# Splitting a first matmul of three chunks into two passes of one and a half, with the hidden layout turned to match

## The chip, the cores and the metric

The kernel runs on one core of one Trainium2 chip. The metric is the device time of that core in microseconds (us). Three runs of the kernel before took 957.19, 957.78 and 957.98 us; the median is 957.78.

The engines are called PE (TensorE, matmuls), PEld (its weight loads), ACT (ScalarE), DVE (VectorE), POOL (GpSimd, which also issues the adding DMAs) and SP (SyncE, which issues loads and stores).

## The reference

The input `x` is (8, 4224, 192). A light convolution with 7 taps per head (8 heads of 24 channels, softmax over the taps) is followed by a block that normalises each row, multiplies by a 192 x 768 weight, takes relu, multiplies by a 768 x 192 weight and adds the row back:

```python
out = np.einsum('hk,bskhg->bshg', w, x_unf)          # 7 causal taps
xn = (x - mu) / np.sqrt(var + 1e-06) * g_ln
ch = np.maximum(xn @ w_ch1, 0.0) @ w_ch2
return (x + ch).astype(np.float32)
```

All arithmetic is fp32. Inputs arrive as 64-bit words in part, which the kernel's first stage converts; the change does not touch that.

## The kernel before

Rows are worked in 18 groups; a full group holds 128 partitions x 16 rows (2048 rows). For each group: taps on ACT (the first two) and DVE (the other five), a 32x32 transpose on DVE (`yt`), the first matmul into the hidden tile, relu, the second matmul, a transpose back, a scale by 1/sigma (ACT) and an addition into the output in DRAM by DMA. Taps of the next group run while this group's matmuls do. Everything is written out in the order in which each engine is to do it (`tc.manual_schedule()`); semaphores are put in wherever two instructions touch the same bytes.

Groups 3 to 17 are the 15 "mixed" groups. In them both matmuls use a Winograd form of Strassen's scheme, with 7 products of quarter matrices instead of 8. The first matmul (`up_mixed`, L611) has rows in two halves and the 768 hidden columns in two halves of three chunks of 128 (`FC = 3`). It multiplies 32-row slices of `yt`: four slices `q` = 0 to 3 run at the same time, each into its own PSUM bank. `rows_of_tiles` (L525) issues them. There are eight PSUM banks; `take_set` (L125) gives four at a time, so there are two sets, X and Y, that take turns.

The three chunks don't fit into one bank of 512 columns (3 x 256 = 768). So the seven products are done in two passes: pass `one` with one chunk (256 columns per bank) and pass `two` with two chunks (512 columns). In each pass the seven products alternate between X and Y. After a product the set is emptied in one of two ways. `evict` (L642) is an ACT copy or relu into the hidden tile. `close` adds a set to what is already in the hidden tile: either DVE adds straight out of PSUM (L648), or ACT evicts into a scratch place and POOL issues an adding DMA from there (L609, `add_by_dma`). Quarters of the hidden tile are called `c11`, `c12`, `c21`, `c22`. Scratch for pass one is the part of `c12` and `c22` that pass two will fill later; scratch for pass two are the rooms `cs` and `tb` of other tiles.

ACT also does the relu of `c11` and `c22` in place (L655). `c12` gets its relu in the eviction, `c21` in `lower_sum` (L806), where DVE also subtracts `c11` from it, as the second matmul needs.

The hidden tile `ht[g]` is one room of SBUF for all groups. In a mixed group its layout is `h e f q j t`: half of rows, half of columns, chunk `f`, slice `q`, then 256 columns. A chunk of a quarter is thus 1024 elements in a row, one run per partition.

The second matmul (`down_fast`, L818) has seven products again (L835). Each runs over three output slices `c`, and for each over chunks in the order 2, 0, 1. It takes six banks one after the other: products called with 0 use `banks[2 * c]`, those called with 1 use `banks[2 * c + 1]`. With X as banks X0 to X3 and Y as Y0 to Y3, the former write X0, X2, Y0 and the latter X1, X3, Y1. After each output slice ACT copies the bank out (L841), and one to three entries of a list `work` follow on ACT: relus that are left, scales of the group before, and the first two taps of the group after the next. Between the products DVE does three `half_sum`s on quarters of the hidden tile (L799).

`ahead` (L981) finishes the group before on DVE (`finish_fast`: addition of two rooms, then transposes), and `up_mixed` calls it between the passes. `pending` is the chain on POOL that works out 1/sigma for two groups (`root`, L450); it is run in two parts from `up_mixed` of the even groups, in POOL's order between the adding DMAs. On DVE the order in `up_mixed` is: `ahead`, 28 tap instructions, `lower_sum` of chunk 2, 3 taps, `close` of `c21`, `lower_sum` of chunks 0 and 1, 9 taps, transpose.

Of the kernel before, what the change touches and what calls it, by code (L numbers as in the profile page):

```python
# [16 lines left out]
def kernel(  # L17
# [475 lines left out]
    def hidden_tile(g):  # L493
        n = groups[g][2]

        if fast[g]:
            ht[g] = room.rearrange(
                "p (h e f q j t) -> p h e f q j t", h=2, e=2, f=FC, q=NQ, t=width(g)
            )
        else:  # L500
            ht[g] = room[:, 0 : NF * NQ * n * C].rearrange(
                "p (f j q t) -> p f j q t", f=NF, q=NQ, t=C
            )
# [5 lines left out]
    def evict_up(g, f, src):  # L509
# [4 lines left out]
        elif width(g) == C:  # L514
            dst = of_products(g)[:, :, f // FC, f % FC].rearrange("p h q j t -> p q h (j t)")
            src = src.rearrange("p q (h w) -> p q h w", h=2)
        else:
            dst = ht[g][:, :, f // FC, f % FC].rearrange("p h q j t -> p q j h t")
# [92 lines left out]
    def up_mixed(g, ahead, pending):  # L611


        W = HJ * C
        last = g + 1 == NG
        assert groups[g][2] == 2 * HJ and PAIR * W == 512 and FC == PAIR + 1
# [3 lines left out]
        s1, s2, s3, s4 = ysums[g]  # L620
        done = groups[g - 1][2]

        class Pass:
            def __init__(self, f0, f1, chain, other):
                self.n, self.chain, self.other = f1 - f0, chain, other
                self.b11, self.b12, self.b21, self.b22 = quarters_of_w1(f0, f1)
                self.t = [v[:, :, P * f0 : P * f1] for v in (w1sums[:, k] for k in range(3))]
                (self.c11, self.c12), (self.c21, self.c22) = [
                    [a[:, h, e, f0:f1].rearrange("p f q j t -> p f q (j t)") for e in range(2)]
                    for h in range(2)  # L630
                ]

            def product(self, to, left, right, first=True, end=True):
                rows_of_tiles(to, left, right, first, end, True)

            def seen(self, banks, f=None):
                src = banks[:, :, 0 : self.n * W] if f is None else banks[:, :, W * f : W * f + W]
                return src.rearrange("p q (f w) -> p f q w", w=W)

            def evict(self, banks, dst, relu=False, f=None):  # L640
                src = self.seen(banks, f)
                nc.scalar.activation(dst, src, AF.Relu) if relu else nc.scalar.copy(dst, src)  # L642

            def close(self, c, banks, part=None, f=None):


                if part is None:
                    nc.vector.tensor_tensor(c, c, self.seen(banks), op=ALU.add)  # L648
                    return
                self.evict(banks, part, f=f)  # L650
                whole = "p f q w -> p (f q w)"
                add_by_dma(c.rearrange(whole), part.rearrange(whole))

            def relu(self, c):
                nc.scalar.activation(c, c, AF.Relu)  # L655

        def parts(pool, tag):

            room = pool.tile([P, J * D], F32, tag=tag, name=f"parts_{tag}{g}")
            return room.rearrange("p (f q w) -> p f q w", q=NQ, w=W)  # L660
# [11 lines left out]
        one, two = Pass(PAIR, FC, X, Y), Pass(0, PAIR, Y, X)  # L672
        p = one
        p.product(X, a11, p.b11, True, False)
        p.evict(X, p.c11)
        p.product(Y, a12, p.b21)
        p.close(p.c11, Y, two.c12[:, 0:1])
        next(pending, None)
        p.product(X, s2, p.t[0], False, False)
        p.evict(X, p.c21)  # L680
        p.product(Y, s3, p.t[1], True, False)
        p.evict(Y, p.c22)
        p.product(X, s1, p.b12, False, False)
        p.close(p.c22, X, two.c12[:, 1:2])
        next(pending, None)
        p.product(Y, a22, p.t[2], False)
        p.close(p.c21, Y, two.c22[:, 0:1])
        p.product(X, s4, p.b22, False)
        p.evict(X, p.c12, True)

        next(ahead)
        p = two
        rooms = parts(cpool, "cs"), parts(bpool, "tb")
        p.product(Y, a11, p.b11, True, False)
        p.evict(Y, p.c11)
        p.product(X, a12, p.b21)
        if last:
            p.close(p.c11, X)
        else:
            for f in range(PAIR):  # L700
# [390 lines left out]
```

## Time and profile before

| | |
|---|---|
| median of the runs | 957.78 us |
| the profiled execution | 959.62 us, span 957.5 us |
| clock granted to PE | 1.0 |
| PE busy | 950.6 us, 99% of the span |
| DVE busy | 890.7 us, 93% |
| ACT busy | 696.6 us, 73% |
| POOL busy | 338.4 us, 35% |
| DMA, queue of POOL | 106.25 MB, 59.8% of 16 engines' span |
| first matmul of one mixed group, in the chain of waits | 27.96 us |
| second matmul of one mixed group, in the chain of waits | 27.44 us |

The page gives, for a group of equal instructions, busy time, mean duration of one in nanoseconds, and the idle time of the engine just before them with what ended it. In a timeline a line has start, duration, engine, line of the kernel, operation, tiles and shapes; a bracket at its end is the idle time before it and the releaser. An fp32 matmul shows as two records. Since four slices run at once, a matmul record lasts longer (374 ns) than the step at which new ones start.

### The profile page before, as it was taken

To read this page: it belongs to the slowest core of one execution; us is meant where nothing else is said; L and a number is where in the kernel's file an instruction comes from. 1 tells how busy PE (TensorE), PEld (TensorE's weight loads), DVE (VectorE), ACT (ScalarE), POOL (GpSimd) and SP (SyncE) were. 2 spreads that over 40 slices of the span, in tenths; PEclk is the share of its full clock that TensorE was granted. 3 is DMA by queue.
4 is the path that set the end of the run, shared out by engine and by line. 5 is a ranking of instruction groups with operands and counts; after the bars stand their busy time and mean duration, and the time that the engine had idled before them with its cause. 6 is when DMAs were issued, how large, how long until landed. Compare 5 with 4: busy or idle time off the path is not lost.

```text
span 957.5 us, 37878 instructions
## 1 busy us (share of the span) xinstructions
PE 950.6 (99%) x16858; PEld 743.1 (78%) x16858; DVE 890.7 (93%) x1489; ACT 696.6 (73%) x1165; POOL 338.4 (35%) x472
## 2 busy tenths in 40 slices
PE   9999999999999999999999999999999999999998
PEld 8998896876869697787968778695867769586787
DVE  7999999999999998999999999999999999999757
ACT  6853678596877959687795968779695877967462
POOL 1058422623145141533227141452316232261310
PEclk9999999999999999999999999999999999999999
DMA  8359589689697988979697896969889696778251
GB/s 204 101 160 212 98 230 280 121 187 229 135 263 138 249 156 181 224 132 277 127 249 151 196 220 127 278 131 252 155 197 205 124 276 132 175 136 138 42 96 68
DMA packets 39544, 168.82 MB, mean 176 GB/s; under 512 B 4437, under 2 KB 8150, under 8 KB 33367
## 3 DMA queue, kind: packets, MB, share of 16 engines
q0 software_dynamic: 32576, 106.25, 59.8%
q1 hardware_dynamic: 6800, 60.16, 17.3%
q8 instruction: 132, 2.16, 0.9%
q14 instruction: 30, 0.25, 0.1%
q10 hardware_dynamic: 6, 0.00, 0.0%
HBM read 38.93 MB, written 50.33 MB: 93 GB/s over the span
## 4 chain that ended last, share of the span: by engine, by line
PE 97%; POOL 1%; DMA 1%; ACT 0%; issue 0%; DVE 0%; ACTq 0%; POOLq 0%
PE ps L533 47%; PE ps L835 44%; PE ps L772 4%; PE ps L367 1%; DMA room<-room 1%; PE ps L326 1%; ACT room L642 0%; POOL room L609 0%; POOL d L460 0%; PE ps L354 0%; POOL r L483 0%; POOL d L479 0%; DVE yt L428 0%; POOL d L478 0%; PE ps L335 0%
## 5 line engine op out<-in xcount | busy, mean ns | idle before, releaser
L417 DVE SCALAR_TENSOR_TENSOR y<-xg,taps,y 128x384 f32<-128x384 f32 (+3 forms) x720 | 364.8, 583 | 1.9 <-DMA y<-room 1.3
L835 PE MATMUL ps<-room,w2sums 128*32 128x256 f32 (+2 forms) x4608 | 247.4, 371 | 0.0
L533 PE MATMUL ps<-yt,w 32*128 32x256 f32 (+2 forms) x4104 | 234.8, 378 | 0.3 <-DVE yt L428 0.3
L642 ACT COPY room<-ps 128x1024 f32<-128x1024 f32 (+1 forms) x135 | 175.0, 1296 | 78.6 <-PE ps L533 77.8
L533 PEld LDWEIGHTS ps<-yt,w 32*128 32x128 f32 x4104 | 204.1, 185 | 25.8 <-issue 8.7
L835 PEld LDWEIGHTS ps<-room,w2sums 128*32 128x32 f32 x4608 | 153.5, 110 | 87.8 <-ACT room L655 5.3
L835 PE MATMUL ps<-room,w 128*32 128x256 f32 (+2 forms) x3456 | 189.8, 371 | 0.1
L802 DVE TENSOR_TENSOR room<-room 128x1024 f32<-128x1024 f32 (+2 forms) x147 | 161.2, 1172 | 22.7 <-PE ps L835 16.1
L835 PEld LDWEIGHTS ps<-room,w 128*32 128x32 f32 x3456 | 113.9, 110 | 67.9 <-DVE room L648 5.0
L533 PE MATMUL ps<-ysums,w1sums 32*128 32x256 f32 x2160 | 125.3, 379 | 0.2 <-issue 0.2
L533 PEld LDWEIGHTS ps<-ysums,w1sums 32*128 32x128 f32 x2160 | 109.1, 185 | 11.2 <-ACT room L642 3.6
L925 POOL DMA_DIRECT2D out_dram<-ot x69 | 58.9, 940 | 159.3 <-ACT ot L914 102.6
L409 POOL DMA_DIRECT2D y<-tb x59 | 52.4, 1384 | 155.0 <-ACT room L841 110.2
L841 ACT COPY cs<-ps 128x256 f32<-128x256 f32 (+2 forms) x192 | 70.2, 367 | 45.6 <-PE ps L835 45.5
L655 ACT ACTIVATE room<-room 128x1024 f32<-128x1024 f32 (+1 forms) x89 | 92.5, 1072 | 0.8 <-DMA room<-parts_cs 0.8
L914 ACT ACTIVATE ot<-ot,r 128x192 f32<-128x192 f32 x224 | 90.9, 464 | 0.0
L380 ACT ACTIVATE y<-xg,taps 128x384 f32<-128x384 f32 (+3 forms) x141 | 73.1, 608 | 0.2 <-DMA xg<-in_x_dram 0.2
L448 DVE BATCH_NORM_STATS2 st<-y 128x6 f32<-128x192 f32 x264 | 70.1, 344 | 0.0
L841 ACT COPY room<-ps 128x256 f32<-128x256 f32 (+2 forms) x96 | 35.5, 369 | 46.5 <-PE ps L835 43.8
L398 ACT ACTIVATE tb<-xg,taps 128x384 f32<-128x384 f32 (+1 forms) x120 | 66.0, 627 | 0.0
L533 PE MATMUL ps<-yt,w1sums 32*128 32x256 f32 x1080 | 65.3, 380 | 0.4 <-ACT room L642 0.4
L533 PE MATMUL ps<-ysums,w 32*128 32x256 f32 x1080 | 64.6, 376 | 0.0
(113 smaller groups left out, 918.0 us busy)
## 6 DMA issues: line engine op xcount, KB each, us to landing
xg<-in_x_dram SPq DMA_DIRECT2D x14, 2112.0 KB, 16.6
room<-room POOLq DMA_DIRECT2D x45, 512.0 KB, 5.1
out_dram<-ot POOLq DMA_DIRECT2D x59, 384.0 KB, 9.6
y<-tb POOLq DMA_DIRECT2D x58, 384.0 KB, 8.5
out_dram<-y SPq DMA_DIRECT2D x13, 1536.0 KB, 9.5
room<-parts_cs POOLq DMA_DIRECT2D x28, 512.0 KB, 6.8
room<-parts_tb POOLq DMA_DIRECT2D x14, 1024.0 KB, 7.6
xg<-in_x_dram POOLq DMA_DIRECT2D x1, 2112.0 KB, 13.6
```

The costliest lines, as they stand in the source:

```text
L380: nc.scalar.mul(y[g][:, 0:n, cs], xg[g][:, 0:n, cs], taps[:, h, 0:1])
L398: nc.scalar.mul(tb[g][:, 0:n, cs], xg[g][:, 1 : 1 + n, cs], taps[:, h, 1:2])
L417: nc.vector.scalar_tensor_tensor(out=y[g][:, 0:n, cs], in0=t[:, k : k + n, cs], scalar=taps[:, h, k : k + 1], in1=y[g][:, 0:n, cs], op0=AL ...
L448: nc.vector.bn_stats(out=sums[g][:, j, :], in_=y[g][:, j, :])
L533: nc.tensor.matmul(banks[:, q, i * w : i * w + w], right[rows, c, P * i : P * i + P], left[rows, :, c, :], start=(first and c == 0 and i = ...
L642: nc.scalar.activation(dst, src, AF.Relu) if relu else nc.scalar.copy(dst, src)
L655: nc.scalar.activation(c, c, AF.Relu)
L802: nc.vector.tensor_tensor(a[:, *dst, f], a[:, *left, f], a[:, *right, f], op=op)
L835: nc.tensor.matmul(dst[C * q : C * q + C, 0:w], right[:, f, C * c : C * c + C], left[:, f, q], start=(first and f == PAIR), stop=(f == PAI ...
L841: nc.scalar.copy(to[:, c], dst[:, 0:w].rearrange("p (j t) -> p j t", t=t))
L914: nc.scalar.mul(ots[g][:, j, :], ots[g][:, j, :], rstd[g][:, j : j + 1])
L925: nc.gpsimd.dma_start(out=rows[:, d0:d1], in_=src[:, d0:d1], accum_op=ALU.add)
```

## The change

Instead of one chunk and then two, each pass now does one and a half chunks: 384 columns per bank. Pass `one` (`Pass(1)`) does chunk 2 in full and half of the rows of chunk 1; pass `two` (`Pass(0)`) chunk 0 and the other half of chunk 1. A product is a matmul of 256 columns and one of 128 for each slice and each part of the contraction. The layout becomes `h e q f j t`, so that a slice's 768 columns lie together, and a pass's part of a quarter is four runs of 384 elements per partition.

Around it:
- Evictions and closings are of 1536 elements, in both passes. The DVE closing is cut into two instructions of two banks each.
- The scratch for closing `c21` in pass one is in the room `cs`, so that `next(ahead)` moves ahead of the closing of `c22`. The second part of `pending` comes behind the adding DMA of `c21`.
- The relu of `one.c11` is cut into six pieces of 256, put behind one eviction each; relus of `two.c11` and `two.c22` are cut by two slices `q`.
- One scale fewer (of two) stands in `up_mixed`; it moves to `work`.
- `lower_sum` goes by the two passes' parts; `close(c21)` and `lower_sum` come ahead of the taps that stood between and before them.
- The six banks of `down_fast` are reordered: products called with 0 use the first three, those called with 1 the last three.
- The two rooms `parts` in `down_fast` lie in chunk 0 of `c21` and of `c22`, slices 0 to 2.

```diff
-                "p (h e f q j t) -> p h e f q j t", h=2, e=2, f=FC, q=NQ, t=width(g)
+                "p (h e q f j t) -> p h e q f j t", h=2, e=2, f=FC, q=NQ, t=width(g)
...
-        W = HJ * C
+        M = HJ * C
+        W = FC * M // 2
...
             def product(self, to, left, right, first=True, end=True):
-                rows_of_tiles(to, left, right, first, end, True)
+                r, n = self.r, left.shape[1] // 2
+                half = left[:, n * r : n * r + n]
+                pieces = [(left, PAIR * r, (W - M) * r, M), (half, 1, M * (1 - r), W - M)]
+                for c in range(CH):
+                    for k, (v, f, w0, w) in enumerate(pieces):
+                        for q in range(NQ):
+                            rows = slice(C * q, C * q + C)
+                            nc.tensor.matmul(
+                                to[:, q, w0 : w0 + w], right[rows, c, P * f : P * f + P],
+                                v[rows, :, c, :], start=(first and c == 0 and k == 0),
+                                stop=(end and c == CH - 1), skip_group_check=True,
+                            )
...
                 if part is None:
-                    nc.vector.tensor_tensor(c, c, self.seen(banks), op=ALU.add)
+                    for q in range(0, NQ, 2):
+                        dst = c[:, q : q + 2]
+                        nc.vector.tensor_tensor(dst, dst, banks[:, q : q + 2, 0:W], op=ALU.add)
                     return
-                self.evict(banks, part, f=f)
-                whole = "p f q w -> p (f q w)"
-                add_by_dma(c.rearrange(whole), part.rearrange(whole))
+                self.evict(banks, part)
+                add_by_dma(c, part)
...
-        one, two = Pass(PAIR, FC, X, Y), Pass(0, PAIR, Y, X)
+        one, two = Pass(1), Pass(0)
...
-        p.close(p.c22, X, two.c12[:, 1:2])
+        next(ahead)
+        p.close(p.c22, X, two.c22)
+        rooms = parts(cpool, "cs"), parts(bpool, "tb")
+        p.product(Y, a22, t[2], False)
+        p.close(p.c21, Y, rooms[0][:, 1])
         next(pending, None)
-        p.product(Y, a22, p.t[2], False)
-        p.close(p.c21, Y, two.c22[:, 0:1])
-        p.product(X, s4, p.b22, False)
+        relu(one.c11, 0, 6)
+        p.product(X, s4, b22, False)
         p.evict(X, p.c12, True)
-
-        next(ahead)
+        relu(one.c11, 1, 6)
+
...
-        if last:
-            p.close(p.c11, X)
-        else:
-            for f in range(PAIR):
-                p.close(p.c11[:, f : f + 1], X, rooms[0][:, f : f + 1], f)
-            if g == 3:
-                store_y(g, nc.gpsimd)
-        act_scales(0, 1)
+        relu(one.c11, 2, 6)
+        p.product(X, a12, b21)
+        p.close(p.c11, X, None if last else rooms[0][:, 0])
+        if g == 3:
+            store_y(g, nc.gpsimd)
+        relu(one.c11, 3, 6)
...
-        p.close(p.c22, Y, None if last else rooms[1][:, 0:PAIR])
-        p.product(X, a22, p.t[2], False)
-        for f in range(PAIR):
-            p.relu(p.c11[:, f : f + 1])
+        p.close(p.c22, Y, None if last else rooms[1][:, 0])
+        act_scales(0, 1)
+        p.product(X, a22, t[2], False)
+        for k in range(2):
+            relu(two.c11, k, 2)
         if last:
-            one.relu(one.c22)
+            relu(one.c22)
         else:
-            lower_sum(g, (PAIR,))
-            taps_of_next(5, 6, heads=(H // 2, H - 1))
+            lower_sum(g, parts_of(g)[0:1])
         p.close(p.c21, X)
...
-        lower_sum(g, range(PAIR))
+        lower_sum(g, parts_of(g)[0 if last else 1 :])
+        taps_of_next(5, 6, heads=(H // 2, H - 1))
...
-        work += [lambda j=j: scale_one(j) for j in range(2, done)]
-        half = [lambda i=i: two.relu(two.c22[:, i : i + 1]) for i in range(PAIR)]
+        work += [lambda j=j: scale_one(j) for j in range(1, done)]
+        half = [lambda k=k: relu(two.c22, k, 2) for k in range(2)]
...
-        free = a[:, 1, 0].rearrange("p f q j t -> p (f q) j t")
-        parts = [free[:, 0:CH], free[:, CH : 2 * CH]]
-        banks = [take_bank() for c in range(CH) for i in range(2)]
+        parts = [a[:, 1, e, 0:CH, 0] for e in range(2)]
+        banks = [take_bank() for i in range(2 * CH)]
+        banks = [banks[c + CH * i] for c in range(CH) for i in range(2)]
```

New functions that it calls:

```python
def relu(c, k=0, n=1):
    m, w = n // 2, W // (n // 2) if n > 1 else W
    c = c if n == 1 else c[:, 2 * (k // m) : 2 * (k // m) + 2, w * (k % m) : w * (k % m + 1)]
    nc.scalar.activation(c, c, AF.Relu)

def parts_of(g):
    a = of_products(g)
    if g not in MIXED or g + 1 == NG:
        return [lambda h, e, f=f: a[:, h, e, :, f] for f in (PAIR, *range(PAIR))]
    w = FC * J * T
    a = a.rearrange("p h e q f j t -> p h e q (f j t)")
    return [lambda h, e, r=r: a[:, h, e, :, w * r // 2 : w * (r + 1) // 2] for r in (1, 0)]
```

## The prediction

> **What bounds the kernel now.** I read the page's busy times first, then the chain of waits, then the two passes of one group as two windows, then who waits for whom, then the engines' timelines around the borders of one group. TensorE (PE) is busy throughout:
>
> ```profile
> PE 950.6 (99%) x16858; PEld 743.1 (78%) x16858; DVE 890.7 (93%) x1489; ACT 696.6 (73%) x1165; POOL 338.4 (35%) x472
> ```
>
> So time comes only from how densely PE is packed. The chain shows each mixed group as two pieces with the same work (504 records of 256 columns, two records to an fp32 matmul):
>
> ```profile
> 452.19 27.96 PE ps L533 x504
> 480.15 27.44 PE ps L835 x504
> ```
>
> The first matmul (L533) takes 0.52 us more than the second (L835). The two windows of one group (microseconds, engine busy time, records) show where:
>
> ```profile
> 452.13:461.74 9.61, 9.61 (x171) 8.16 (x169) 9.47 (x20) 6.45 (x7) 2.77 (x3) 1.00 0.73 139
> 461.74:480.08 18.34, 18.34 (x340) 17.12 (x336) 17.13 (x28) 13.98 (x12) 3.47 (x4) 1.00 0.73 138
> ```
>
> The one-chunk pass has half the work of the two-chunk pass, but 9.61 is 0.44 over half of 18.34. Its products last 1.3 us, and ScalarE (ACT) can hardly empty a bank set in that:
>
> ```profile
> 399.40 1.01 ACT L642 COPY room<-ps 128x1024 f32<-128x1024 f32 x1 [0.28 <-PE ps L533]
> ...
> PEld ps L533 <- ACT room L642: 11.4, 46, 0.8
> PEld ps L835 <- ACT room L655: 5.3, 14, 0.4
> ACT room L655 <- DMA room<-parts_cs: 0.8, 2, 0.6
> ```
>
> The other two waits matter below. The border between two groups:
>
> ```profile
> 452.12 0.74 PEld L533 LDWEIGHTS ps<-yt,w 32*128 32x128 f32 x16 [0.41 <-issue]
> 452.13 0.93 PE L533 MATMUL ps<-yt,w 32*128 32x256 f32 x12
> 452.24 0.37 ACT L841 COPY cs<-ps 128x256 f32<-128x256 f32 x1 [0.92 <-PE ps L835]
> ```
>
> The new group's first matmul starts while the last copy out of the second matmul's banks has still to run. That is possible because this copy reads a bank of set Y.
>
> **The change part by part**, for 15 mixed groups. Products are numbered 1 to 7 (pass one), 8 to 14 (pass two) and D1 to D7 (second matmul).
>
> *A, more and narrower matmuls.* Each product is now 12 matmuls of 256 columns and 12 of 128; records per group go from 504 to 672. Four records run at once. The trace's records show a step of four every 215.8 ns at 256 columns and every 162.5 ns at 192 (the first `up`). A line through both gives 109.2 for 128, 1.3 more than half a 256 step. The nearest row with its own load per 128-column record is the last four of L367, stepping 109 to 112. 84 such steps per group cost 84 x 1.3 = 0.11 to 84 x 2.8 = 0.24 us: 1.6 to 3.5 us, below which no row points. I take 2.5. That a load (185 ns) would set the pace is excluded by the 162.5.
>
> One rule speaks against this. The Trainium skill, "TensorE: Matmul & The Clock Gate", section "Back-to-back issue gap", says a stream of load and matmul pairs sustains about 81 ns at 128 columns, where the isolated formula gives 56. Scaled by that ratio (an estimate) a step would be 158 ns, 49 more, and the sum 62 us higher; the L367 row is the measurement and does not show it.
>
> *B, the waits of the short pass.* Counted on single record starts of one group, six borders of pass one are late by 120, 62, 57, 136, 48 and 125 ns: 0.548 us. A product now lasts 6 x 215.8 + 6 x 110 = 1.955 us. Evictions of 1024 and 2048 elements take 1.01 and 1.87, so 1536 take 1.44. A set must be emptied between a product's end (0.16 us after the next begins), plus 0.09 to start ACT, 1.44, 0.05 for the semaphore and 0.11 for the load: 1.85 of 1.955. So the waits go, with a margin of 0.1 us: 15 x 0.548 = 8.2. One group also waits 0.7 us (at 751 us) for the DMA that reads scratch in `c22`; that DMA now leaves before the variance chain on GpSimd (POOL). Together -8.9 (bounds: -8.9, and -4 if half of it returns).
> What is late next: the small relus of `one.c11`, 0.3 us each behind an eviction, fit in the 0.5 us that ACT has left per product.
>
> *C, the bank order.* The product with `banks[2*c]` ran in X0, X2, Y0; it now runs in X0, X1, X2. D7 is such a product, so its last copy reads X2, and the next group's first product writes X0 to X3 at once. Its third record must wait: copy end 452.61, 0.05 semaphore, 0.11 load, so 452.77 instead of 452.23. PE issues in order, so all of it is lost: 0.54 x 15 = 8.0 us. It is nothing only if product 1 began later for another reason (bounds 0 and +8.2). At the other border nothing is gained: D1 begins as the last matmul drains.
>
> *D, the addition that closes `two.c11`.* In the old layout these DMAs move 128 runs of 4,096 bytes; with `q` outside the chunks a quarter's half is four runs of 1,536 bytes per partition, 512 runs. Rows around that:
>
> ```profile
> L609 POOL DMA_DIRECT2D room<-parts_cs x28 | 24.0, 870 | 46.6 <-ACT parts_cs L642 45.9
> L409 POOL DMA_DIRECT2D y<-room x2 | 3.2, 1901 | 9.8 <-ACT y L380 9.8
> room<-room POOLq DMA_DIRECT2D x45, 512.0 KB, 5.1
> ```
>
> 128 runs cost 0.87 us of POOL, 1024 runs (L409 `y<-room`, 144-float rows) at least 1.6: I take 1.2. Packets of 1,536 bytes take 140 ns on this queue, 32 per engine: 4.5 us against 2.77. From issue to first packet 1.44 us now, 1.77 then; completion 0.4. So 6.65 us from issue to landing, and about 0.5 more where a 16 KB instruction packet (0.95 us) holds up one of the 16 engines.
> Product 9 now ends five products of 1.955 before the second matmul (it was five of 2.6). From the first matmul of a group: it ends at 17.75, eviction to 19.28, POOL 0.30 later (as at 400.42 to 400.72): issue 19.58, landing 26.2 to 26.7. In even groups POOL first works off the rest of the variance chain (6.3 us from DMA issue to DMA issue, 404.84 to 411.15), which now stands after the `c21` DMA of 13.72: issue 20.33, landing 27.0 to 27.5.
> The second matmul begins at 27.48. Its third step, 0.43 later, needs both halves of relu(`two.c11`): 1.6 us after landing, and 0.12 for semaphores and load. So the wait is landing + 1.72 - 27.91: 0.04 to 0.54 in odd groups, 0.79 to 1.29 in even ones. Middles 0.29 and 1.04, seven groups each: 9.3 us. Bounds: 0 (the old lead of the DMA: only 2 of 14 relus waited, 0.8 us in all, so there is nothing to gain) and +16 (an engine late by 1.4, as at 422.2 in the trace).
> Queued on ACT behind the waiting relus are the eviction of product 14 and D1's copies; PE waits for them only after it has waited for the relus.
>
> *E, D3.* It needs relu(`two.c22`), for which PE waits 0.11 us per group now (the L655 row). The halves are now cut by `q`, so the second chunk read needs both, 0.43 sooner, while ACT reaches their end 0.4 sooner: with ACT pushed by D, 0.1 more per group, 1.5 us. Bounds 0 and 4 (in group 3 a 1.5 MB store goes ahead of the `c22` DMA).
>
> *F, last group.* VectorE (DVE) closes `c11` and `c22` itself; two additions of 768 at 0.92 against products of 1.955 leave 0.25 us over, twice: 0.5 (0 to 1).
>
> *Nothing for the rest.* DVE: `lower_sum` and `half_sum` keep their elements in fewer instructions; the closing of `c21` goes ahead of four taps (2.1 us). Its cover is D1 to D3 (11.6 us), which hold 1.7 + 12 x 0.53 + 3.38 = 11.5 of work: it just suffices, and half a microsecond more would still meet D5. One more scale moves into the second matmul, 0.35 us of ACT, paid by the shorter eviction before it. `next(ahead)` moves over one eviction; DVE is done with it 6.9 us into the group and `two.c22` is written at 10. The SP queue is passed by nothing; its store waits 1 to 2 us longer for the taps and feeds nothing near.
>
> Sum: 2.5 - 8.9 + 8.0 + 9.3 + 1.5 + 0.5 = +12.9 us. The profiled execution took 959.62 (span 957.5 and 2.1 around it), so 972.5 for one like it; it stands 1.84 over the median of 957.78, which gives 970.7.
>
> **The rivals.**
> 1. *The addition lands in time* (D near 0, E 0.5): only 2 relus ever waited. Against it: the lead shrinks by 3.2 us and the transfer grows by 2. 957.78 + 2.5 - 8.9 + 8.0 + 0.5 + 0.5 = 960.4.
> 2. *Faster: product 1 does not meet the copy and the landing is hidden.* The mechanism is PE's drain at the border: if the new group's third record starts after 452.66 anyway, C is 0. For it: the load there is released by "issue", not by a wait; against it: 452.23. With D 0: 952.4. It decides as soon as C and D together stay under 5 us.
> 3. *C is hidden but D is paid*: 962.7, or 958 if only even groups pay half.
> 4. *The 128-column loads or the 0.1 us margin of B fail*: waits of pass one return in all 14 borders, about +0.5 us a group over the forecast: 978.
>
> **How the numbers follow.** Forecast 0.45; rival 1 0.25; rival 2 0.12; rival 3 0.09; rival 4 0.09. The measurement can tell about 0.2%, 1.9 us: under 955.9 is faster, over 959.7 slower. Faster: rival 2 and a little of 1 and 3, 0.13. Same: the edges of rivals 1 and 3, 0.09. Slower: 0.78. The forecast's own range is 965 to 978 (D from 4 to 16). The whole range takes in rivals 1, 3 and most of 4: 957.5 to 979.
>
> **What would show it.** L533's successor with 672 records per group in the chain, 19,378 PE records in all; two windows of equal length in a group; no wait of its loads for the 128x1536 evictions (B). A wait of PEld for ACT L841 at each group's start, about 0.4 to 0.5 us (C). ACT waiting for `room<-parts_cs` some 10 us in total, POOL DMA issues of 1.2 us and 1,536-byte packets (D). If that DMA wait is below 2 us, D was wrong; if the group's start is dense, C was; if a 128-column step takes over 115 ns, A was.

## The result, and the profile after

The changed kernel takes 1002.97 us (median of 4 runs, 1002.44 to 1006.57), the kernel before 957.88 in the same session: 1.048 times as long, 95% interval 1.0455 to 1.0505. I had predicted 970.7 with a range of 957.5 to 979.0. The direction was right; the size was 32 us short. The profiled execution of the changed kernel, from which the lines below are, took 1006.57 us, 3.6 over the median.

The page of the changed kernel: busy times, two of its DMA queues, POOL's issues of adding DMAs and the time to landing of those out of `cs`:

```profile
PE 969.9 (97%) x19378; PEld 803.8 (80%) x19378; DVE 881.4 (88%) x1450; ACT 711.6 (71%) x1226; POOL 367.4 (37%) x458
q0 software_dynamic: 58592, 110.70, 65.2%
q8 instruction: 152, 2.49, 0.9%
L609 POOL DMA_DIRECT2D room<-room x30 | 39.1, 1303 | 105.1 <-ACT room L652 104.2
room<-parts_cs POOLq DMA_DIRECT2D x29, 768.0 KB, 9.6
```

The kernel before has for the instruction queue and for the last row:

```profile
q8 instruction: 132, 2.16, 0.9%
room<-parts_cs POOLq DMA_DIRECT2D x28, 512.0 KB, 6.8
```

PE has its 19,378 records and is busy for 97% instead of 99%, in a span of 1004.8 us: 35 us without work, where there were 7. q8 carries instructions: 152 packets of 16,384 bytes, 132 before. The shares of DVE and ACT have fallen (from 93 and 73%), and POOL's went from 35 to 37%, so none of them became the bound.

The chain of waits, two consecutive groups of the changed kernel (start, length, engine, line, records). L644 is the first matmul, L853 the second:

```profile
472.23 23.06 PE ps L644 x461
495.76 5.58 PE ps L644 x96
502.52 0.50 PE ps L644 x6
503.02 27.57 PE ps L853 x504
530.59 21.81 PE ps L644 x464
554.46 5.52 PE ps L644 x110
561.23 1.69 PE ps L644 x27
```

Before, 12 of the 15 first matmuls took 27.96 us each, the others at most 28.65. These two are broken in two places each and last 30.8 and 32.3 us; the second matmul takes 27.57 us, against 27.44. (The chain counts only those records that it passes, so its counts do not add up to 672.) Who waits for whom, in total:

```profile
PEld ps L644 <- issue: 37.2, 42, 2.8
PE ps L644 <- issue: 24.0, 21, 2.6
ACT room L668 <- DMA room<-parts_cs: 18.0, 11, 3.3
PEld ps L853 <- ACT room L668: 6.4, 14, 0.7
PEld ps L644 <- ACT cs L859: 3.6, 15, 0.2
```

"issue" means that PE waited for nothing that the profile shows: no engine, no DMA of the program. (The two "issue" rows of L644 are mostly the same moments, seen by the loads and by the matmuls.) The forecast had no term for it. The kernel before has such a row too, of 11.8 us with no wait longer than 0.6 us (it is shown with *runs* below). PE's timeline over the two breaks of the second of these groups:

```profile
549.72 2.68 PE L644 MATMUL ps<-ysums,w1sums 32*128 32x256 f32 x59
554.46 1.03 PE L644 MATMUL ps<-ysums,w1sums 32*128 32x128 f32 x18 [2.06 <-issue]
...
559.16 0.83 PE L644 MATMUL ps<-yt,w 32*128 32x256 f32 x14
561.23 1.69 PE L644 MATMUL ps<-yt,w 32*128 32x128 f32 x34 [1.24 <-issue]
```

PE stops in the middle of a product, whose operands and banks it already has. The instruction packets of q8 in the trace explain it. Around these two breaks they are (us; worked out from the trace's DMA records):

```
packet 552.23 - 553.16     PE works again at 554.46, 1.30 after its end
packet 559.02 - 560.06     PE works again at 561.23, 1.17 after its end
```

Count a break from the start of one TensorE instruction to the start of the next. Over the whole run, 22 breaks of more than 0.5 us end 1.1 to 1.7 us after an instruction packet has ended, 32.5 us in all; 19 of them lie in first matmuls. In the kernel before there is one such break, of 0.6 us.

How late a block may be can be counted. The trace holds 38,876 records of PE's queue (38,756 of matmuls and loads, 120 of semaphores and drains) and 152 packets, 255.8 records to a packet: a packet is 256 instructions. When packet i (from 0) starts, PE has begun 256 i + n instructions, where n goes from about 156 in the calmest part to 449. The value 449 is a wall: in the changed kernel and in split, oldbanks and quiet below the largest n is exactly 449, and no kernel here passes it.

The breaks stand at that place and nowhere else. In each of the 22 the instruction at which PE resumes is number 256 i + 449 (from 0), where i is the packet that has just come; between the two breaks shown above PE starts 128 matmuls and 128 loads, one block. The same holds for every break of the mixed groups in the kernels below, except one of the two in *runs*. A wait for data or for a bank would not keep to a count of instructions: PE has run out of them and waits for the next block.

So from n = 156 on there are 293 instructions left until packet i must have come. In the old first matmul (1,008 instructions in 27.96 us) they last 8.1 us, in the new one (1,344 in 28.25 when nothing breaks it, as in some groups of *slab* below) 6.2.

The Trainium skill, "Runtime: NRT & Kernel Launch", section "Instruction fetch mechanics", says that an engine's instructions come through a first-in-first-out store, filled in blocks of 16 KiB, 256 instructions, by a DMA queue of the sequencer, and that the cost of a block's border is mostly hidden. The trace agrees on the block (255.8 records) and on the queue (q8). On "mostly hidden" it agrees for the kernel before (one break, 0.6 us) and not for this one (32.5 us).

### The profile page after: what moved, and what is told of

It reads as the page before. It is cut to its first block, busy times and chain, and to the rows that moved or that the text cites. A ratio compares the mean times of both kernels' runs of the same rounds, so it can differ in the third digit from the quotient of the medians.

```text
span 1004.8 us, 42796 instructions
## 1 busy us (share of the span) xinstructions
PE 969.9 (97%) x19378; PEld 803.8 (80%) x19378; DVE 881.4 (88%) x1450; ACT 711.6 (71%) x1226; POOL 367.4 (37%) x458
## 4 chain that ended last, share of the span: by engine, by line
PE 46%; issue 4%; DVE 2%; DMA 2%; POOL 1%; ACT 0%; POOLq 0%; DVEq 0%
PE ps L853 24%; PE ps L644 22%; DVE room L823 2%; DMA room<-parts_cs 1%; DMA room<-room 1%; PE ps L783 1%; POOL room L609 0%; POOL ysums L605 0%; POOL yt L606 0%; DVE cs L893 0%; DVE ysums L601 0%; DVE ysums L600 0%; ACT room L652 0%; ACT room L668 0%; DVE y L947 0%
## 5 line engine op out<-in xcount | busy, mean ns | idle before, releaser
L853 PE MATMUL ps<-room,w2sums 128*32 128x256 f32 (+2 forms) x4608 | 255.8, 371 | 0.1
L652 ACT COPY room<-ps 128x1536 f32<-128x1536 f32 x120 | 172.6, 1439 | 97.5 <-PE ps L644 83.6
L853 PEld LDWEIGHTS ps<-room,w2sums 128*32 128x32 f32 x4608 | 169.6, 110 | 75.9 <-ACT room L668 2.8
L644 PE MATMUL ps<-yt,w 32*128 32x256 f32 (+1 forms) x4320 | 201.5, 326 | 9.6 <-issue 9.3
L644 PEld LDWEIGHTS ps<-yt,w 32*128 32x128 f32 x4320 | 188.3, 186 | 22.6 <-issue 17.8
L853 PE MATMUL ps<-room,w 128*32 128x256 f32 (+2 forms) x3456 | 202.8, 371 | 2.5 <-issue 1.9
L853 PEld LDWEIGHTS ps<-room,w 128*32 128x32 f32 x3456 | 126.1, 110 | 63.5 <-ACT room L668 3.5
L823 DVE TENSOR_TENSOR room<-room 128x1536 f32<-128x1536 f32 (+2 forms) x102 | 156.1, 1600 | 17.7 <-ACT cs L859 8.5
L644 PE MATMUL ps<-ysums,w1sums 32*128 32x128 f32 (+1 forms) x2880 | 134.2, 328 | 12.4 <-issue 12.3
L644 PEld LDWEIGHTS ps<-ysums,w1sums 32*128 32x128 f32 x2880 | 126.8, 188 | 15.4 <-issue 15.1
L668 ACT ACTIVATE room<-room 128x256 f32<-128x256 f32 (+2 forms) x164 | 107.0, 672 | 21.7 <-DMA room<-parts_cs 18.0
L830 DVE SCALAR_TENSOR_TENSOR room<-room 128x1536 f32<-128x1536 f32 (+1 forms) x31 | 51.9, 1680 | 69.8 <-ACT room L668 60.8
L609 POOL DMA_DIRECT2D room<-room x30 | 39.1, 1303 | 105.1 <-ACT room L652 104.2
L644 PE MATMUL ps<-ysums,w 32*128 32x256 f32 (+1 forms) x1440 | 70.8, 324 | 2.6 <-issue 2.5
L644 PEld LDWEIGHTS ps<-ysums,w 32*128 32x128 f32 x1440 | 66.3, 186 | 4.6 <-issue 4.3
```

The source lines that it names most:

```text
L644: nc.tensor.matmul(to[:, q, w0 : w0 + w], right[rows, c, P * f : P * f + P], v[rows, :, c, :], start=(first and c == 0 and k == 0), stop=( ...
L823: nc.vector.tensor_tensor(part(*dst), part(*left), part(*right), op=op)
L853: nc.tensor.matmul(dst[C * q : C * q + C, 0:w], right[:, f, C * c : C * c + C], left[:, q, f], start=(first and f == PAIR), stop=(f == PAI ...
```

## The experiments

Eleven kernels in three submissions. Beside each ratio stands the median of the kernel before in the same submission.

**First submission: short runs, instruction count, or both; and the bank order by itself.** Two things had changed that could delay instructions: the adding DMAs' runs (128 of 4,096 bytes became 512 of 1,536) and PE's instructions per first matmul (1,008 became 1,344).

*runs*: the kernel before, with five of six adding DMAs of a group as 512 runs of 1,024 bytes, by a scratch with gaps.

```diff
+                if c.shape[1] == 1:
+                    add_by_dma(c[:, 0], part[:, 0])
+                    return
...
-            return room.rearrange("p (f q w) -> p f q w", q=NQ, w=W)
+            order = "p (q f w) -> p f q w" if tag == "cs" else "p (f q w) -> p f q w"
+            return room.rearrange(order, q=NQ, w=W)
...
-        p.close(p.c11, Y, two.c12[:, 0:1])
+        p.close(p.c11, Y, spread(two.c12, 0))
...
```

> The kernel before with one thing else: five of the six adding DMAs of a group read a scratch with gaps, so that each moves 512 runs of 1,024 bytes instead of 128 of 4,096 (the one that closes c22 in pass two keeps 128 long runs). Matmuls and banks stay. Theory 'runs' alone: gaps of PE after instruction packets appear here too, at the old instruction count, and cost some 10 to 35 us: 968 to 993. Theory 'rate': none appear, 957 to 961. If it takes both (late packets, and more of them needed), this kernel shows few gaps, 957 to 964, and 'slab' shows few as well.

Measured: 968.55 us (967.12 to 968.82) against 956.73, ratio 1.0117 (1.01 to 1.0134). PE's and ACT's waits in this kernel:

```profile
PEld ps L533 <- ACT room L642: 21.2, 52, 2.8
PEld ps L533 <- issue: 11.8, 45, 0.6
ACT room L642 <- DMA room<-room: 10.4, 7, 2.7
```

The 11.8 us with "issue" are the kernel before's own, word for word. The loss is another wait: in even groups the eviction of product 12 into `c22` (L642) waits for the slower DMA that still reads its scratch there, and PE for the eviction; product 12 takes 3.2 to 5.1 us in seven groups instead of 2.59. So short runs at the old instruction count do not starve PE; they lengthen transfers, and that can cost elsewhere. The time lies at the edge of what theory 'runs' gave (968 to 993), but by this other mechanism.

*slab*: the changed kernel, with a hidden layout in which the half quarter that one pass writes lies in one piece, so that an adding DMA has 128 runs of 6,144 bytes. *slab_oldbanks* is the same with the kernel before's bank order.

```diff
-        if fast[g]:
+        if slab(g):
+            ht[g] = room.rearrange("p (h e r q w) -> p h e r q w", h=2, e=2, r=2, q=NQ)
+        elif fast[g]:
...
+                if slab(g):
+                    c, part = [v.rearrange("p q w -> p (q w)") for v in (c, part)]
                 add_by_dma(c, part)
...
```

In both, the partial sums of the second matmul of two groups (the one before the first mixed group and the one before the last group) lie where the next group writes early, and are overwritten before they are added, so the output of these groups is wrong; the work done is the same. slab2_oldbanks below puts them elsewhere.

> The changed kernel with one thing else: the hidden tile of groups 3 to 16 is laid out h e r q w (r the pass), so that a pass's part of a quarter is one run of 1536 elements per partition, and each adding DMA moves 128 runs of 6,144 bytes instead of 512 of 1,536. Matmuls, their order and the banks stay. Theory 'runs' (PE's instruction packets of 16 KB come late because they stand behind the short runs on the same 16 DMA engines): the gaps of PE over 0.5 us that end about 1.4 us after such a packet, 24 of them now, fall to the 1 or 2 of the kernel before, and the time falls to 957.9 + 4.7 (narrower matmuls) - 8.2 (waits of the short pass) + 8.1 (bank order) + 0 to 3 = 960 to 966. Theory 'rate' (PE simply uses up instructions faster than they can be brought, 1344 per first matmul instead of 1008): the gaps stay, 990 to 1003.

> As 'slab', with the bank order of the kernel before. Theory 'runs' and the step of the bank order: 8 us less than 'slab', 952 to 958, which would be at or under the kernel before. Theory 'rate': 982 to 995.

Measured: 976.77 (976.43 to 979.13), ratio 1.0212 (1.0197 to 1.0228); 973.9 (968.76 to 975.91), ratio 1.0169 (1.0137 to 1.0201). The breaks that follow an instruction packet are 8 with 6.3 us and 15 with 13.1 us, against 22 with 32.5. Both theories miss, in both kernels: the times lie between theirs. So long runs remove most of the loss but not all, and the count of instructions must have a part of its own.

*banks*: the kernel before with the new bank order alone.

```diff
-        banks = [take_bank() for c in range(CH) for i in range(2)]
+        banks = [take_bank() for i in range(2 * CH)]
+        banks = [banks[c + CH * i] for c in range(CH) for i in range(2)]
```

> The kernel before with only the new bank order of the second matmul. The step of the prediction: the first product of the next group waits for the last copy out of X2, 0.54 us per group, 15 groups: 957.9 + 8.1 = 966. If the wait hides in PE's change of tiling at the border: 958.

Measured: 964.48 (963.47 to 965.97), ratio 1.008 (1.0065 to 1.0095). One row is new among PE's waits, once per mixed group:

```profile
PEld ps L533 <- ACT cs L842: 3.8, 15, 0.3
```

At a group's start the timeline of the loads has it here:

```profile
509.26 0.30 PEld L533 LDWEIGHTS ps<-yt,w 32*128 32x128 f32 x4 [0.41 <-issue]
509.82 1.82 PEld L533 LDWEIGHTS ps<-yt,w 32*128 32x128 f32 x36 [0.26 <-ACT cs L842]
```

The first load of the group starts, the second comes 0.56 us later and waits for the last copy out of the second matmul's bank. Product 1 takes 1.75 instead of 1.40 and product 2 1.49 instead of 1.31: 0.53 us per group, 7.9 us for 15; the medians differ by 7.75.

**Second submission: the instruction count by itself, and the other parts undone in the changed kernel.**

*split*: the kernel before, in which the second chunk of the long pass is written as two matmuls of 128 columns. The instructions per first matmul are 1,344; layout, DMAs and banks are the kernel before's.

```diff
-                for q in range(NQ):
...
-                        left[rows, :, c, :], start=(first and c == 0 and i == 0),
...
+                n = left.shape[1]
+                cut = [(0, n // 2), (n // 2, n)] if split and i else [(0, n)]
+                for j1, j2 in cut:
+                    for q in range(NQ):
...
+                            right[rows, c, P * i : P * i + P], left[rows, j1:j2, c, :],
...
```

> The kernel before, in which the second chunk of each long product is written as two matmuls of 128 columns instead of one of 256: the first matmul of a mixed group then has the 1,344 TensorE instructions that the changed kernel has, and layout, adding DMAs and bank order stay. The narrower matmuls themselves cost what they cost in the changed kernel, 22.5 ns for each of 14 products in 15 groups, 4.7 us: 961.5. Theory that the number of instructions by itself starves TensorE (the fetch of 256 instructions has 293 instructions' time to come in, 7.6 us at the old pace and 6.0 us at the new one): stalls as in the two kernels with long runs, 8 to 16 of over 0.5 us in the first matmuls, 970 to 980 us. Theory that the short runs of the adding DMAs are needed for it: no such stall, 960 to 964 us.

Measured: 985.98 (982.8 to 991.32) against 957.57, ratio 1.0306 (1.0268 to 1.0344): 28 us more, beyond what either theory gave. A group without a break, in the chain:

```profile
176.78 28.27 PE ps L536 x672
```

PE's timeline around two breaks of another group, the second of them in the second matmul (L839):

```profile
658.02 1.71 PE L536 MATMUL ps<-yt,w1sums 32*128 32x256 f32 x40
661.60 1.27 PE L536 MATMUL ps<-yt,w1sums 32*128 32x128 f32 x28 [1.87 <-issue]
...
665.54 1.50 PE L839 MATMUL ps<-room,w 128*32 128x256 f32 x24
669.35 3.15 PE L839 MATMUL ps<-room,w 128*32 128x256 f32 x32 [2.30 <-issue]
```

And the waits:

```profile
PEld ps L536 <- issue: 23.6, 56, 2.1
PEld ps L839 <- issue: 15.5, 21, 2.8
```

Unbroken, the group costs 0.31 us more than before (28.27 against 27.96): that is the price of the narrower matmuls, 4.7 us for 15 groups. The rest is breaks: 9 in first matmuls (12.1 us) and 8 in the first two products of the second (11.5 us), all ending 1.3 to 1.5 us after an instruction packet. The second matmul's own instructions are unchanged; that it starts with a store of instructions that the first has run down is my reading of it. The instruction count alone is thus enough to starve PE.

*oldbanks*: the changed kernel with the old bank order (the edit of *banks*, reversed).

> The changed kernel with the kernel before's order of the PSUM banks in the second matmul. If the wait for the last copies out of PSUM adds to the rest, 15 times 0.54 us come off: 995 us. If a pause at the start of a group gives the fetch of instructions time that is then missing elsewhere, part of the gain goes into stalls, as between the two kernels with long runs, which differ by 2.9 us: 997 to 1001 us.

Measured: 1004.54 (1002.25 to 1006.69), ratio 1.0494 (1.0469 to 1.0519). The wait for the copy is gone from PE's list, and product 1 is back from 2.41 to 2.07 us. The time has not moved, further even than the second expectation: the breaks after instruction packets are now 27 with 38.1 us. What the group's start gives back, the next blocks of instructions seem to take: the breaks have 5.7 us more, the starts 6.4 less.

*quiet*: the changed kernel without the DMAs that add a group's result to the output in the mixed groups.

```diff
-            if j == 7:
-                add_to_out(g - 1, 0, 8)
-            elif j == done - 1:
-                add_to_out(g - 1, 8, done)
```

> The changed kernel without the DMAs that add a group's result to the output in the mixed groups (the output then lacks the second matmul's part for 14 groups): 21 MB of 110 MB that the software queue moves. TensorE's instructions are the changed kernel's. If a fetch is late because it waits behind data in the DMA engines, the median wait of 3.8 us (95% within 6.8 us) falls towards the kernel before's 3.3 (5.6), at most 12 of the 24 stalls of the first matmuls are left, and the time is 972 to 988 us. If the fetch is late for another reason (its own pace, TensorE's), stalls and time stay: 998 to 1004 us.

Measured: 999.51 (999.33 to 1002.05), ratio 1.0451 (1.0426 to 1.0476). The queue moves 21 MB less, as intended, and the time is no more than 3.5 us less:

```profile
q0 software_dynamic: 50672, 89.27, 53.2%
```

PE's largest wait remains:

```profile
PEld ps L644 <- issue: 31.7, 40, 2.5
```

The expectation by the DMA load, 972 to 988, fails: 22 breaks with 27.3 us are left.

*slab2_oldbanks*: *slab_oldbanks* with the partial sums of those two groups in a place that the next group writes last.

```diff
+        if slab(min(g + 1, NG - 1)):
+            v = room.rearrange("p (h e r q w) -> p h e r q w", h=2, e=2, r=2, q=NQ)
+            parts = [
+                v[:, 1, e, 0, 0:CH, 0:w].rearrange("p q (j t) -> p q j t", t=t)
+                for e in range(2)
+            ]
```

> The changed kernel with a hidden layout in which the half that a pass writes is one run of 6,144 B on each partition, so that an adding DMA has 128 runs, and with the old order of the banks; in two groups the partial sums of the second matmul lie where the next group writes last. By the first run of this form 969 to 976 us, with 10 to 17 stalls over 0.5 us. If the stalls of that form came from short runs alone there should be none: 961 us.

Measured: 970.64 (969.71 to 974.21), ratio 1.0147 (1.0122 to 1.0173). It does the whole computation and is the best form of the new passes found; the kernel before stays faster. Its waits:

```profile
PEld ps L650 <- issue: 20.6, 38, 1.7
ACT room L676 <- DMA room<-parts_cs: 10.5, 11, 2.0
PEld ps L887 <- ACT room L676: 2.7, 8, 0.5
```

Its group of DMA issues on POOL (line, busy us, mean ns, idle before):

```profile
L614 POOL DMA_DIRECT2D room<-parts_cs x29 | 25.8, 888 | 56.1 <-ACT parts_cs L658 56.0 <-issue 0.2
```

Against oldbanks, with the same instructions and the same bank order, the layout with long runs is worth 33.9 us (where the second matmul reads and leaves its partial sums moves with it). An issue on POOL is back at 0.89 us, the wait of the second matmul for the relu falls from 6.4 us (in the changed kernel) to 2.7, and the breaks fall to 14 with 12.6 us.

**Third submission: is it a threshold?** *split_third* and *split_two* cut only one or two of the three column blocks (`if split and i and c == 0`, `c < 2` in the line above): 1,120 and 1,232 instructions. *split_quiet* is split without the DMAs into the output, as in quiet.

> The kernel before with a third of the edit called split: of the second chunk's matmuls in the long passes only those of the first of three column blocks are cut in two, 1,120 TensorE instructions in a first matmul of a mixed group in place of 1,008 (split has 1,344 and took 985.98). The narrower matmuls cost a third of 4.7 us. Theory of a threshold (a fetch is late only if it comes later than the 293 instructions last, here 7.3 us instead of 8.1): by the waits of the kernel before one fetch is late, 0.6 us in all: 959 to 962 us. Theory that each further instruction costs the same: a third of 28 us, 967 us.

> The same with two of the three blocks: 1,232 instructions, the narrower matmuls cost 3.1 us. Threshold: 293 instructions last 6.7 us; by the waits of the kernel before 2 fetches are late, by those of split 5, with 1.5 to 2.6 us in all: 962 to 968 us. In proportion: 976 us.

> The kernel split without the DMAs that add a group's result to the output in the mixed groups (the output lacks the second matmul's part for 14 groups). In the changed kernel the same cut took 3.5 us off. If the fetches wait for their turn in the DMA engines, and the adding DMAs of short runs were what filled them there, the cut takes more off here, where the other DMAs have long runs: 964 to 976 us. If the wait does not depend on the other traffic: 983 to 988 us.

Measured, against 957.14: split_third 960.6 (959.48 to 962.17), ratio 1.0036 (1.0024 to 1.0049); split_two 966.21 (964.6 to 968.98), ratio 1.0097 (1.0073 to 1.0121); split_quiet 983.45 (982.18 to 985.67), ratio 1.0282 (1.0263 to 1.0301). Waits of the second matmul's loads, in split_third and split_two (both L839), where split has 15.5:

```profile
PEld ps L839 <- issue: 2.6, 5, 1.3
```

```profile
PEld ps L839 <- issue: 7.2, 11, 1.5
```

The first two fall where the threshold had them (959 to 962, 962 to 968) and not in proportion (967, 976). The third is again a miss for the DMA load: 2.5 us for 21 MB, which is less than split's own runs differ by.

All of it in one table. "Time" is a difference of medians; "groups", "breaks" and "wait" are of the profiled execution, which was the longest of the changed kernel's runs and of split's and the shortest of those of quiet and split_quiet. "Groups" is the time of the 15 mixed groups in the profiled execution over that of the kernel before (827.0 us); "breaks" are those over 0.5 us in these groups that end 1.1 to 1.7 us after an instruction packet; "wait" is the time from n = 156 to the start of the packet, median and 95th percentile over the packets of these groups (the expectation of quiet has medians up to 0.4 us higher).

| kernel | instructions | adding runs | time over before, us | groups, us | breaks | wait, us |
|---|---|---|---|---|---|---|
| before | 1,008 | 128 | 0 | 0 | 1, 0.6 us | 2.9, 5.5 |
| banks | 1,008 | 128 | +7.8 | +6.6 | 1, 0.6 us | 2.7, 5.1 |
| runs | 1,008 | 512, 1 KB | +11.8 | +9.4 | 2, 1.4 us | 3.0, 5.1 |
| split_third | 1,120 | 128 | +3.5 | +2.1 | 2, 2.0 us | 3.0, 5.1 |
| split_two | 1,232 | 128 | +9.1 | +9.5 | 8, 7.3 us | 3.2, 5.8 |
| split | 1,344 | 128 | +28.4 | +32.1 | 17, 23.6 us | 3.4, 6.0 |
| split_quiet | 1,344 | 128 | +26.3 | +24.7 | 16, 17.3 us | 2.7, 5.6 |
| slab | 1,344 | 128 | +20.0 | +19.7 | 8, 6.3 us | 3.2, 5.4 |
| slab_oldbanks | 1,344 | 128 | +17.2 | +15.5 | 15, 13.1 us | 3.3, 5.1 |
| slab2_oldbanks | 1,344 | 128 | +13.1 | +16.9 | 14, 12.6 us | 3.6, 5.4 |
| changed | 1,344 | 512, 1.5 KB | +45.1 | +48.2 | 22, 32.5 us | 3.7, 6.7 |
| oldbanks | 1,344 | 512, 1.5 KB | +47.0 | +46.9 | 27, 38.1 us | 3.5, 6.9 |
| quiet | 1,344 | 512, 1.5 KB | +41.9 | +41.3 | 22, 27.3 us | 3.0, 6.3 |

Two things decide whether a block is late: how long the 293 instructions last (8.1 us at 1,008 per first matmul, 7.3, 6.7 and 6.2 at the counts below it), and how long the fetch takes to start. A fetch needs its wait, 0.95 us for the packet and about 1.4 until PE works. With the old pace 8.1 - 2.35 = 5.8 us of wait are free, which over 95% of the old waits stay within; with the new one 3.8, which is about the median of the changed kernel's waits (3.7).

These are means over a first matmul. The kernels with split in their name have all their extra instructions in pass two, and by its products 293 instructions last 7.9 us there in the kernel before, 6.8 in split_third, 6.0 in split_two and 5.4 in split (96, 112, 128 and 144 instructions in 2.59, 2.605, 2.62 and 2.635 us); in the changed kernel they last 6.0 us in both passes (96 in 1.965). So over pass two split asks for more than the changed kernel ever does, and its 23.6 us of breaks are not the changed kernel's share of the count. The nearest to that share are the 12.6 us of slab2_oldbanks, which has the changed kernel's own instructions and long runs. That the denser pass is why split breaks more was not tried by itself.

What stays open: what a fetch waits for. It is not simply the amount of other DMA traffic: without 21 MB of it the median wait is 0.7 us shorter in both pairs (quiet, split_quiet), and the time hardly falls. And 512 short runs lengthen the late waits at 1,344 instructions (6.3 to 6.9 against 5.4) but not at 1,008 (5.1), where the runs are of 1,024 bytes and fall at other times. The records do not tell which of the 16 DMA engines a packet used.

## Why the prediction was wrong

**The step that failed is "Nothing for the rest".** It went through DVE, ACT's extra scale, POOL and the SP queue, and did not count PE's supply of instructions. A third more instructions in a first matmul were costed in A by their execution only, and D has the 16 KB instruction packet as something that holds up an adding DMA, not as something that can itself come late. In their place the runs showed breaks of PE at the borders of instruction blocks: in the changed kernel 32.5 us in breaks over 0.5 us and 3.6 us in ten of 0.1 to 0.5 us at the same place. The count of instructions is enough to cause them (split: 28.4 us, of which 4.7 are execution and nearly all the rest breaks); with the changed kernel's own instructions and long runs (slab2_oldbanks) they are 12.6 us, and the layout with short runs brings them to 32.5 and 38.1. The page of before had the row to ask about: its q8 line counts 132 packets, and the first matmul used up a packet every 7 us.

Without the breaks the forecast comes nearer, by misses in both directions. From the products of undisturbed groups, a product takes 1.965 us, and:

- **A**, +2.5 forecast (1.6 to 3.5): 1.965 against half of 1.295 + 2.590, 22.5 ns for 14 products in 15 groups, 4.7 us, outside its bounds. A 128-column step takes 112 ns. The L367 row, 109 to 112, had that, but the upper bound was worked out with 110.7. Split gives the same 0.31 us per group. The rule that I weighed there, the Trainium skill's "TensorE: Matmul & The Clock Gate", section "Back-to-back issue gap", scaled to 158 ns a step (an estimate), is not what the runs show, as the L367 row had said.
- **B**, -8.9 forecast: right. An undisturbed first matmul of slab_oldbanks or slab2_oldbanks takes 27.72 us, against 14 x 1.965 = 27.51, so 0.21 us of wait are left of 0.76. That is -8.3, and with the 0.7 us of the one group whose eviction waited for a DMA (no such wait is left) -9.0.
- **C**, +8.0 forecast: right in mechanism and, in banks, in size (7.75). In the changed kernel the start of a group costs 0.43 us: product 1 takes 2.41 against 2.07, product 2 2.05 against 1.97; 6.4 us. Another 0.2 us at the border from the second matmul to the first is in every group of the changed kernel, 2.8 us, and stays there with the old bank order; I don't know its cause. The border in the changed kernel:

```profile
530.52 0.30 PEld L644 LDWEIGHTS ps<-yt,w 32*128 32x128 f32 x4 [0.41 <-issue]
530.64 0.37 ACT L859 COPY cs<-ps 128x256 f32<-128x256 f32 x1 [0.92 <-PE ps L853]
531.06 2.28 PEld L644 LDWEIGHTS ps<-yt,w 32*128 32x128 f32 x56 [0.24 <-ACT cs L859]
```

  The load of the third step starts 0.05 us after the copy's end, as forecast. But undoing C alone did not help: in oldbanks the breaks grew by about as much.
- **D**, +9.3 forecast (0 to 16): the mechanism is there, the size was a third. The issue takes 1.30 us on POOL (1.2 forecast), the median from issue to landing is 9.6 us (6.65 forecast; the kernel before already took 6.8 with its 128 runs, so the forecast was too short by a row of its own page), yet product D1 is late by only 4.8 us in all, in five groups, and 2.1 of these are breaks that end after an instruction packet, so D cost 2.7 us. The group with the fewest breaks before it (the one at 181 us) loses 0.85 to D, near the 1.04 of the forecast for even groups; in most others the breaks of the first matmul come before D1 and give the DMA the time that it lacks. That this is why D is small was not tried. With 128 runs (slab2_oldbanks) D1 is late by 1.1 us in all, 0.6 of it a break.
- **E**, +1.5, and **F**, +0.5: nothing that can be told from the rest.

A, B, C, the border and D sum to 4.7 - 9.0 + 6.4 + 2.8 + 2.7 = +7.6 us, against +12.9 in the forecast. The mixed groups of the profiled execution are 48.2 us longer; of the other 40.6, 32.5 are breaks over 0.5 us, 3.6 shorter ones, and 4.5 I could not place. None of the four rivals had this mechanism. Rival 4 came nearest with 978, by waits that did not return. That the direction came out right owes little to the sum: its parts make up 7.6 of the 48.2 us.

The signs that I named were there: the record count, the wait for the copy at a group's start (15 waits, 3.6 us on top of the load's usual start), POOL's issue time, ACT's wait of 18.0 us for `room<-parts_cs` (10 forecast). The passes of a broken group are not equal, since most breaks lie in products 7 to 14.

## What to carry to other kernels

Where PE is busy for 97 to 99%, its instructions are a resource with a rate: before cutting matmuls smaller, divide the span's instructions by the packets of the instruction queue and compare how long a block lasts with how long its fetch takes in the trace (here, as means over a first matmul, 8.1 us held, 7.3 and 6.7 began to break, and at 6.2 13 of the changed kernel's 15 groups broke). Look at the densest stretch, not only at the mean. A gap with the releaser "issue" in the middle of a product is the sign. An instruction packet that ends 1.1 to 1.7 us before PE resumes confirms it, and breaks that always come at the same place in the count of instructions are the proof. A gain elsewhere in such a stretch can be lost again: undoing the bank order returned 6.4 us to the start of the changed kernel's groups and none to its time, and with long runs 2.9 us of some 8 (slab against slab_oldbanks).

## What the runs showed of the hardware that was not expected

- A PE instruction block of 256 instructions, 16,384 bytes, takes 0.95 us as a DMA packet (median), and after a break PE worked again 1.1 to 1.7 us after its end, mostly 1.3 to 1.5. PE never got past instruction 256 i + 449 before packet i had come, and every break of the mixed groups but one came there.
- The cost grows much faster than the count: in the split kernels +11% instructions cost 3.5 us, +22% 9.1, +33% 28.4, of which the execution itself is 1.6, 3.1 and 4.7.
- The loss spreads: split's runs lie between 982.8 and 991.3, those of the kernel before between 955.6 and 958.7. And it is paid later than it is caused: 8 of split's 17 breaks are in the second matmul, whose instructions had not changed.
- Taking 21 MB out of 110 MB from the queue of adding DMAs moved a starved kernel by 3.5 us or less, while a layout that turns 512 runs of 1,536 bytes into 128 of 6,144 at equal bytes moved it by 33.9. Why, stays open.
